# Attention on one core: loads in chunks of 4 heads over a ring of 8, value loads from ScalarE's queue, smaller and later stores

## The chip, the cores and the metric

The kernel runs on one core of a Trainium2 chip. A core has five engines with instruction streams of their own: TensorE (PE) multiplies matrices into PSUM, VectorE (DVE) and ScalarE (ACT) read PSUM and SBUF, GpSimd (POOL) works on SBUF, and SyncE (SP) here only sends DMAs. They meet through semaphores. DMAs are sent by an engine's queue and carried out by 16 DMA engines that all queues share. The metric is the device time of one execution in microseconds (us), as a median over runs.

## The reference

```python
B, H, Sq, Sk, D = 16, 32, 192, 1024, 128          # all bf16
scores = jnp.einsum("bhqd,bhkd->bhqk", q, k) * D ** -0.5
p = softmax(scores, axis=-1)
out = jnp.einsum("bhqk,bhkd->bhqd", p, v)
```

There are 512 independent heads. Each has 192 queries, 1024 keys and 1024 values of 128 elements. In bytes: a head's keys and its values are 262 KB each, its queries and its output 49 KB each; the whole problem moves 318.8 MB.

## The kernel before

**Units.** Two heads form a pair, and a pair is worked off as three units of 128 query rows: the first 128 queries of head a (k3 = 0), the first 128 of head b (k3 = 1), and the last 64 of both together (k3 = 2, two matmuls side by side in the array). That makes 256 pairs and NU = 768 units. `PPG` is the number of pairs in a group of G = 16 heads (8), `UPG` the number of units (24), and there are NGR = 32 groups.

**Stages of a unit u.** QK (`qk`, L215 to L228): two times 512 keys into a PSUM tile `s_ps`. Row maximum (`rowmax`, L300, VectorE): it writes the negated scaled scores to `ss` in SBUF and their minimum to `nb`. Then the route of the unit decides: for k3 = 0 and 1 (route W) GpSimd subtracts the minimum (`shift`, L188) into `x_sb`, and the exponential is taken later; for k3 = 2 (route EA) ScalarE takes the exponential (`exp_first`, L356) into `x_sb` and sums the row. Eight transposes on TensorE (`tr`, L244) put `x_sb` into a PSUM tile `pt_ps`. ScalarE evacuates it into `pt_sb` (`evac`, L367 with the exponential for route W, L369 as a copy for route EA). PV (`pv`, L267 to L281) multiplies by the values into `o_ps`; for route W further matmuls with a column of ones sum the rows (L270). After a pair's third unit VectorE normalises (`onorm`, L327, L330) into `ob`.

**Order.** The order on each engine is written out by hand as a loop over steps, with a lag for each stage: `LAGS=(2, 4, 5, 7)` are L_X, L_TR, L_EV, L_PV. In step s TensorE does QK of unit s + 1, the transposes of unit s - 4, and PV of unit s - 7; ScalarE evacuates unit s - 5 and then does `exp_first` of unit s - 2. Two tiles each of `s_ps`, `pt_ps` and `o_ps` fill PSUM. So the transposes of unit u wait for the evacuation of unit u - 2, and an evacuation waits for the transposes of its unit and for PV of unit u - 4 (`s_pv`, through the NPT = 4 slots of `pt_sb`).

**Loads and stores.** All DMAs are sent by SP (lines 133 to 174). `kt`, `qt` and `vs` each have NS = 2 slots of 16 heads. `loads(g)` sends three DMAs: the keys through a transposing DMA (L141), the queries through another (L144), and the values as a plain load (L149, runs of 2 KB). From the third group on, L141 waits until QK has finished with the group two before (`s_qk`), and L149 until PV has (`s_pv`). `stores(g)` waits until the 8 pairs of a group are normalised (`s_on`) and sends three stores: the first 128 rows of each head (L158), and the last 64 rows of the even and of the odd heads (L163, L164). `ob` has NSO = 2 slots of 16 heads, and `onorm` waits for the store that used the slot before. SP's order is loads of groups 0 and 1, and then for each g: loads of g + 2, stores of g. TensorE waits for the keys and the queries at the first QK of a group (L203, L204) and for the values at its first PV (L251).

Of the kernel before, what the change touches and what calls it, by code (L numbers as in the profile page):

```python
# [5 lines left out]
BF16 = mybir.dt.bfloat16  # L6
# [4 lines left out]
R_EA = 0  # L11
R_ED = 1
R_W = 2


def _attention_kernel(nc, q, k, v, out, G=16, NS=2, LAGS=(2, 4, 5, 7), ROUTES=(R_W, R_W, R_EA)):
    B, H, SQ, D = q.shape
    SK = k.shape[2]
    assert D == 128 and SK == 1024 and SQ == 192, (D, SK, SQ)
    NH = B * H  # L20
    assert NH % G == 0 and G % 2 == 0
    NGR = NH // G
    PPG = G // 2
    UPG = 3 * PPG
    NU = NGR * UPG
    KT_TILES = SK // 128
    scale = float(D) ** -0.5

# [2 lines left out]
    NSS = L_X + 2  # L31
    NX = L_TR - L_X + 2
    NPT = L_PV - L_EV + 2
    NSO = 2
    NRS = 4

    qf = q.rearrange("b h s d -> (b h) s d")
# [25 lines left out]
    with ExitStack() as es:  # L63
        def sb(name, shape, dt):
            return es.enter_context(nc.sbuf_tensor(name, shape, dt))
# [4 lines left out]
        def sem(name):  # L70
            return es.enter_context(nc.semaphore(name))

        kt = sb("kt", [128, NS, G * SK], BF16)
        qt = sb("qt", [128, NS, G * SQ], BF16)
        vs = sb("vs", [128, NS, G, KT_TILES, 128], BF16)
        ob = sb("ob", [128, NSO, PPG, 4, 128], BF16)
        ss = sb("ss", [128, NSS, SK], F32)
        nb = sb("nb", [128, NSS], F32)
        x_sb = sb("x_sb", [128, NX, SK], BF16)
# [6 lines left out]
        pt_ps = [ps("pt_ps%d" % i, [128, KT_TILES, 128], BF16) for i in range(2)]  # L86
        o_ps = [ps("o_ps%d" % i, [128, 4, 128], F32) for i in range(2)]
        s_setup = sem("s_setup")
        sxk = [sem("sxk%d" % i) for i in range(NS)]
        sxq = [sem("sxq%d" % i) for i in range(NS)]  # L90
# [15 lines left out]
        def unit_info(u):  # L106
            pr = u // 3
            k3 = u % 3
            g = pr // PPG
            pg = pr % PPG  # L110
            return pr, k3, g, pg

        O_SLOT = (0, 2, 1)

        def load_cnt(g):
            return 16 * (g // NS + 1)

        def store_cnt(g):
            return 48 * (g // NSO + 1)
# [12 lines left out]

        @block.sync
        def _(e):
            def loads(g):
                s = g % NS
                last_u = (g - NS + 1) * UPG - 1
                h0 = g * G
                if g >= NS:
                    e.wait_ge(s_qk, last_u + 1)  # L140
                e.dma_start_transpose(  # L141
                    kt[:, s], kf[h0:h0 + G].rearrange("g k d -> (g k) d")
                ).then_inc(sxk[s], 16)
                e.dma_start_transpose(  # L144
                    qt[:, s], qf[h0:h0 + G].rearrange("g k d -> (g k) d")
                ).then_inc(sxq[s], 16)
                if g >= NS:
                    e.wait_ge(s_pv, last_u + 1)
                e.dma_start(  # L149
                    vs[:, s], vf[h0:h0 + G].rearrange("g (p t) d -> p g t d", t=KT_TILES)  # L150
                ).then_inc(svl[s], 16)

            def stores(g):
                so = g % NSO
                e.wait_ge(s_on, (g + 1) * PPG)
                h0 = g * G
                og = of[h0:h0 + G]
                e.dma_start(  # L158
                    og[:, 0:128, :].rearrange("h p d -> p h d"),
                    ob[:, so].rearrange("p pg (x y) d -> p (pg x) (y d)", y=2)[:, :, 0:128],  # L160
                ).then_inc(sst[so], 16)
                oab = og[:, 128:192, :].rearrange("(pg x) p d -> x p pg d", x=2)
                e.dma_start(oab[0], ob[0:64, so, :, 1, :]).then_inc(sst[so], 16)  # L163
                e.dma_start(oab[1], ob[64:128, so, :, 1, :]).then_inc(sst[so], 16)  # L164

            for g in range(min(NS, NGR)):
                loads(g)
            for g in range(NGR):
                if g + NS < NGR:
                    loads(g + NS)  # L170
                stores(g)
            for so in range(min(NSO, NGR)):
                n_uses = len(range(so, NGR, NSO))
                e.wait_ge(sst[so], 48 * n_uses)

        @block.gpsimd
# [21 lines left out]
        def _(pe):  # L198
            def qk(u):
                pr, k3, g, pg = unit_info(u)  # L200
                s = g % NS
                if u % UPG == 0:
                    pe.wait_ge(sxk[s], load_cnt(g))  # L203
                    pe.wait_ge(sxq[s], load_cnt(g))  # L204
                if u >= 2:
                    pe.wait_ge(s_max, u - 1)
                S = s_ps[u % 2]
                a = 2 * pg
                b = 2 * pg + 1
                ins = None  # L210
                for c in range(2):
                    cs = slice(512 * c, 512 * c + 512)
                    if k3 < 2:
                        x = a if k3 == 0 else b
                        ins = pe.matmul(  # L215
                            S[:, cs],
                            qt[:, s, x * SQ: x * SQ + 128],
                            kt[:, s, x * SK + 512 * c: x * SK + 512 * c + 512],
                            start=True, stop=True,
                        )  # L220
# [13 lines left out]
                ins.then_inc(s_qk, 1)  # L234
# [12 lines left out]
            def pv(u):  # L247
                pr, k3, g, pg = unit_info(u)
                s = g % NS
                if u % UPG == 0:  # L250
# [44 lines left out]
        def _(dve):  # L295
# [15 lines left out]
            ri_total = [0]  # L311

            def onorm(pr):
                g = pr // PPG
                pg = pr % PPG
                so = g % NSO
                dve.wait_ge(s_pv, 3 * pr + 3)
                if pg == 0 and g >= NSO:
# [29 lines left out]
        def _(act):  # L348
# [13 lines left out]
            def evac(u):  # L362
                act.wait_ge(s_tr, u + 1)
                if u >= NPT:
                    act.wait_ge(s_pv, u - NPT + 1)
                if route(u) == R_W:
                    act.activation(pt_sb[:, u % NPT], pt_ps[u % 2][:], ACT_FN.Exp, scale=-1.0).then_inc(s_eva, 1)  # L367
                else:
                    act.activation(pt_sb[:, u % NPT], pt_ps[u % 2][:], ACT_FN.Copy).then_inc(s_eva, 1)  # L369

            for step in range(NU + L_EV + 1):
                u = step - L_EV
                if 0 <= u < NU and route(u) != R_ED:
                    evac(u)
                u = step - L_X
                if 0 <= u < NU and route(u) != R_W:
                    exp_first(u)
# [38 lines left out]
```

## Time and profile before

| | |
|---|---|
| median of 3 runs | 1265.64 us (1265.32 to 1267.57) |
| profiled execution, first to last instruction | 1263.1 us |
| between the two | 2.5 us |
| TensorE busy | 1234.2 us (98%) |
| VectorE busy | 1102.0 us (87%) |
| ScalarE busy | 1048.6 us (83%) |
| GpSimd busy | 960.4 us (76%) |
| granted TensorE clock, mean | 0.999 of full speed |
| DMA, mean over the span | 255 GB/s |

The page gives the span of the profiled execution, not its whole device time, so sums in this document are made against the span, and the 2.5 us between it and the median of the runs are carried over unchanged.

A row of instructions reads: line, engine, operation, output tile and input, shape and count, then busy time, mean duration, and the idle time of the engine ahead of it with what ended it. `PEld` is TensorE's loading of weights, which overlaps its matmuls. In a timeline the first column is the start and the second the duration, both in us from the start of the span; `x8` says that eight instructions are merged. Rows of `SPq` are SP's queue: the duration is how long the issue of the DMA held the queue, not the time until the data have landed. In the table of windows the columns are: window, length, busy time of PE, PEld, DVE, ACT and POOL with their instruction counts, TensorE's granted clock, DMA share (sum of packet times over 16 engines; over 1 where packets overlap), and GB/s.

### The profile page before, as it was taken

What the parts mean: (1) busy time and instruction counts of PE and PEld (TensorE: products, weight loads), DVE (VectorE), ACT (ScalarE), POOL (GpSimd) and SP (SyncE); (2) the same over time, 40 slices, a digit from 0 to 9 for tenths busy, and PEclk for the clock granted to TensorE, in tenths of its full rate; (3) what the DMA queues carried; (4) which work ended last, traced back from release to release, by engine and by line L of the source; (5) the groups of instructions that cost most, each with busy time, mean ns of one, the idle gap of its engine ahead of it and who ended that gap; (6) DMA issues with size and microseconds to landing.
All of it is one profiled execution on the core that took longest, in us unless ns stands there. A gap on an engine that the chain in (4) does not pass through costs nothing.

```text
span 1263.1 us, 48658 instructions
## 1 busy us (share of the span) xinstructions
PE 1234.2 (98%) x20480; PEld 1009.4 (80%) x20480; DVE 1102.0 (87%) x2304; ACT 1048.6 (83%) x1281; POOL 960.4 (76%) x518
## 2 busy tenths in 40 slices
PE   3999999999999999999999999999999999999997
PEld 1888888888888888888888888888888888888886
DVE  2889888898988989898898988889898898989885
ACT  1888888888888888888888888888888888888886
POOL 2778777777877778787777877777787777878774
PEclk9999999999999999999999999999999999999999
DMA  9999999999999999999999999999999999999941
GB/s 288 268 261 240 278 280 266 288 270 245 254 269 261 279 233 255 281 275 262 261 230 272 271 276 268 252 251 272 272 267 281 253 263 252 271 261 281 244 118 27
DMA packets 790743, 321.89 MB, mean 255 GB/s; under 512 B 724992, under 2 KB 724992, under 8 KB 790528
## 3 DMA queue, kind: packets, MB, share of 16 engines
q1 hardware_dynamic: 790528, 318.78, 108.8%
q8 instruction: 164, 2.69, 0.8%
q14 instruction: 51, 0.42, 0.1%
HBM read 134.22 MB, written 25.17 MB: 126 GB/s over the span
## 4 chain that ended last, share of the span: by engine, by line
PE 97%; SPq 1%; DMA 1%; ACT 0%; issue 0%; DVE 0%; ACTq 0%
PE pt_ps L244 33%; PE o_ps L267 24%; PE s_ps L215 18%; PE o_ps L273 11%; PE s_ps L222 9%; SPq L141 1%; DMA vs<-in_v_dram 1%; PE o_ps L270 1%; PE o_ps L275 1%; SPq L144 0%; PE s_ps L228 0%; ACT x_sb L356 0%; ACT pt_sb L367 0%; DVE ob L330 0%; DVE rinv L327 0%
## 5 line engine op out<-in xcount | busy, mean ns | idle before, releaser
L188 POOL TENSOR_TENSOR x_sb<-ss,nb 128x1024 bf16<-128x1024 f32 x512 | 959.7, 1895 | 288.9 <-PE pt_ps L244 266.8
L300 DVE TENSOR_SCALAR_CACHE_REDUCE ss<-s_ps 128x1024 f32<-128x1024 f32 x768 | 938.5, 1222 | 140.5 <-PE s_ps L215 110.8
L244 PEld LDWEIGHTS pt_ps<-ident,x_sb 128*128 128x128 bf16 x6144 | 487.1, 148 | 203.3 <-issue 105.4
L367 ACT ACTIVATE pt_sb<-pt_ps 128x1024 bf16<-128x1024 bf16 x512 | 521.0, 1018 | 41.9 <-PE pt_ps L244 41.8
L244 PE MATMUL pt_ps<-ident,x_sb 128*128 128x128 bf16 x6144 | 520.7, 228 | 0.2 <-ACT pt_sb L367 0.2
L267 PE MATMUL o_ps<-vs,pt_sb 128*128 128x128 bf16 x4096 | 403.0, 217 | 0.3 <-DMA vs<-in_v_dram 0.3
L369 ACT ACTIVATE pt_sb<-pt_ps 128x1024 bf16<-128x1024 bf16 x256 | 262.1, 1024 | 140.1 <-PE pt_ps L244 140.0
L270 PE MATMUL o_ps<-ones,pt_sb 128*128 128x1 bf16 x4096 | 376.0, 165 | 0.0
L267 PEld LDWEIGHTS o_ps<-vs,pt_sb 128*128 128x128 bf16 x4096 | 352.3, 97 | 0.5 <-DMA vs<-in_v_dram 0.4
L270 PEld LDWEIGHTS o_ps<-ones,pt_sb 128*128 128x128 bf16 x4096 | 340.7, 96 | 0.0
L215 PE MATMUL s_ps<-kt,qt 128*128 128x512 bf16 x1024 | 305.3, 379 | 21.3 <-DMA qt<-in_q_dram 21.0
L356 ACT ACTIVATE x_sb<-ss,nb 128x1024 bf16<-128x1024 f32 x256 | 292.3, 1142 | 23.6 <-DVE ss L300 23.6
L273 PE MATMUL o_ps<-vs,pt_sb 128*64 128x128 bf16 x2048 | 162.3, 222 | 0.0
L275 PE MATMUL o_ps<-vs,pt_sb 128*64 128x128 bf16 x2048 | 162.3, 222 | 0.0
L222 PE MATMUL s_ps<-kt,qt 128*64 128x512 bf16 x512 | 153.2, 381 | 0.6 <-DVE ss L300 0.5
L228 PE MATMUL s_ps<-kt,qt 128*64 128x512 bf16 x512 | 153.2, 381 | 0.0
L330 DVE TENSOR_TENSOR ob<-o_ps,rinv 128x384 bf16<-128x384 f32 x256 | 142.7, 557 | 8.7
L273 PEld LDWEIGHTS o_ps<-vs,pt_sb 128*64 128x64 bf16 x2048 | 121.0, 109 | 17.1
L275 PEld LDWEIGHTS o_ps<-vs,pt_sb 128*64 128x64 bf16 x2048 | 121.0, 109 | 0.0
L215 PEld LDWEIGHTS s_ps<-kt,qt 128*128 128x128 bf16 x1024 | 63.3, 96 | 23.6 <-issue 21.5
L300 DVE DVE_READ_ACCUMULATOR ss<-s_ps 128x1 f32 x768 | 64.0, 83 | 0.0
L356 ACT ACTIVATION_READ_ACCUMULATOR x_sb<-ss,nb 128x1 f32 x256 | 48.9, 191 | 0.0
(11 smaller groups left out, 165.7 us busy)
## 6 DMA issues: line engine op xcount, KB each, us to landing
vs<-in_v_dram SPq DMA_DIRECT2D x32, 4096.0 KB, 15.2
out_dram<-ob SPq DMA_DIRECT2D x32, 512.0 KB, 15.9
out_dram<-ob SPq DMA_DIRECT2D x64, 128.0 KB, 4.9
kt<-in_k_dram SPq DMA_TRANSPOSE x32, 21.4
qt<-in_q_dram SPq DMA_TRANSPOSE x32, 6.6
```

The lines of the kernel that those rows point to most:

```text
L188: gp.tensor_tensor(x_sb[:, u % NX, :], ss[:, u % NSS, :], nb[:, u % NSS: u % NSS + 1].to_broadcast([128, SK]), ALU.subtract,).then_inc(s_x ...
L215: ins = pe.matmul(S[:, cs], qt[:, s, x * SQ: x * SQ + 128], kt[:, s, x * SK + 512 * c: x * SK + 512 * c + 512], start=True, stop=True,)
L222: pe.matmul(S[0:64, cs], qt[:, s, a * SQ + 128: a * SQ + 192], kt[:, s, a * SK + 512 * c: a * SK + 512 * c + 512], start=True, stop=True, ...
L244: ins = pe.transpose(PT[:, t, :], X[:, t: SK: KT_TILES], ident[:])
L267: ins = pe.matmul(O[:, sl, :], PTS[:, t, :], vs[:, s, x, t, :], start=first, stop=last, skip_group_check=True)
L270: ins = pe.matmul(O[:, 3, sl: sl + 1], PTS[:, t, :], ones[:, 0:1], start=False, stop=last, skip_group_check=True)
L273: pe.matmul(O[0:64, sl, :], PTS[:, t, 0:64], vs[:, s, a, t, :], start=first, stop=last, skip_group_check=True, tile_position=(0, 0))
L275: ins = pe.matmul(O[64:128, sl, :], PTS[:, t, 64:128], vs[:, s, b, t, :], start=first, stop=last, skip_group_check=True, tile_position=(0, ...
L300: dve.tensor_scalar(ss[:, u % NSS, :], s_ps[u % 2][:], -scale, None, ALU.mult, ALU.min, accum_out=nb[:, u % NSS: u % NSS + 1],).then_inc(s ...
L356: act.activation(x_sb[:, u % NX, :], ss[:, u % NSS, :], ACT_FN.Exp, bias=nb[:, u % NSS: u % NSS + 1], scale=-1.0, accum_out=rs[:, pr % NRS ...
L367: act.activation(pt_sb[:, u % NPT], pt_ps[u % 2][:], ACT_FN.Exp, scale=-1.0).then_inc(s_eva, 1)
L369: act.activation(pt_sb[:, u % NPT], pt_ps[u % 2][:], ACT_FN.Copy).then_inc(s_eva, 1)
```

## The change

The slots become smaller and more: chunks of CH = 4 heads (PPC = 2 pairs, UPC = 6 units) in a ring of NS = 8 slots, so the buffers are as large as before (32 heads), and there are NCH = 128 chunks. Keys and queries of a chunk are still sent by SP, now counted on one semaphore per slot; from chunk 8 on, SP waits until QK has finished with chunk c - 8. Values are sent by ScalarE, between its evacuation and its `exp_first` in a step: chunk c < 8 at step 3(c - 1), at least 0, without a wait; a later chunk at step 6(c - 7) + 8, directly behind the evacuation that waited for the same count of `s_pv`. Stores are for SG = 8 heads (PPS = 4 pairs) with a ring of NSO = 3; SP sends a store group after the load of a chunk once the chunk it waited for lies far enough behind the pairs of the group, and the remaining groups after the last load. TensorE's wait for keys and queries is one wait every 6 units, that for values likewise.

```diff
-def _attention_kernel(nc, q, k, v, out, G=16, NS=2, LAGS=(2, 4, 5, 7), ROUTES=(R_W, R_W, R_EA)):
+def _attention_kernel(nc, q, k, v, out, CH=4, NS=8, SG=8, NSO=3, LAGS=(2, 4, 5, 7), ROUTES=(R_W, R_W, R_EA)):
...
-        kt = sb("kt", [128, NS, G * SK], BF16)
-        qt = sb("qt", [128, NS, G * SQ], BF16)
-        vs = sb("vs", [128, NS, G, KT_TILES, 128], BF16)
-        ob = sb("ob", [128, NSO, PPG, 4, 128], BF16)
+        kt = sb("kt", [128, NS, CH * SK], BF16)
+        qt = sb("qt", [128, NS, CH * SQ], BF16)
+        vs = sb("vs", [128, NS, CH, KT_TILES, 128], BF16)
+        ob = sb("ob", [128, NSO, PPS, 4, 128], BF16)
...
         @block.sync
         def _(e):
-            def loads(g):
-                s = g % NS
-                last_u = (g - NS + 1) * UPG - 1
-                h0 = g * G
-                if g >= NS:
-                    e.wait_ge(s_qk, last_u + 1)
+            def load_kq(c):
+                s = c % NS
+                h0 = c * CH
+                if c >= NS:
+                    e.wait_ge(s_qk, (c - NS + 1) * UPC)
                 e.dma_start_transpose(
-                    kt[:, s], kf[h0:h0 + G].rearrange("g k d -> (g k) d")
-                ).then_inc(sxk[s], 16)
+                    kt[:, s], kf[h0:h0 + CH].rearrange("g k d -> (g k) d")
+                ).then_inc(sx[s], 16)
                 e.dma_start_transpose(
-                    qt[:, s], qf[h0:h0 + G].rearrange("g k d -> (g k) d")
-                ).then_inc(sxq[s], 16)
-                if g >= NS:
-                    e.wait_ge(s_pv, last_u + 1)
-                e.dma_start(
-                    vs[:, s], vf[h0:h0 + G].rearrange("g (p t) d -> p g t d", t=KT_TILES)
-                ).then_inc(svl[s], 16)
+                    qt[:, s], qf[h0:h0 + CH].rearrange("g k d -> (g k) d")
+                ).then_inc(sx[s], 16)
...
-            for g in range(min(NS, NGR)):
-                loads(g)
-            for g in range(NGR):
-                if g + NS < NGR:
-                    loads(g + NS)
-                stores(g)
+            done = 0
+            for c in range(NCH):
+                load_kq(c)
+                while done < NSG and UPC * (c - NS + 1) >= 3 * PPS * (done + 1) + L_PV + 2:
+                    stores(done)
+                    done += 1
+            while done < NSG:
+                stores(done)
+                done += 1
...
-                if u % UPG == 0:
-                    pe.wait_ge(sxk[s], load_cnt(g))
-                    pe.wait_ge(sxq[s], load_cnt(g))
+                if u % UPC == 0:
+                    pe.wait_ge(sx[s], 2 * load_cnt(g))
...
+            def load_v(c):
+                s = c % NS
+                if c >= NS:
+                    act.wait_ge(s_pv, (c - NS + 1) * UPC)
+                act.dma_start(
+                    vs[:, s],
+                    vf[c * CH:(c + 1) * CH].rearrange("g (p t) d -> p g t d", t=KT_TILES),
+                ).then_inc(svl[s], 16)
+
+            v_at = {}
+            for c in range(NCH):
+                at = 3 * (c - 1) if c < NS else (c - NS + 1) * UPC - 1 + NPT + L_EV
+                v_at.setdefault(max(at, 0), []).append(c)
+
             for step in range(NU + L_EV + 1):
                 u = step - L_EV
                 if 0 <= u < NU and route(u) != R_ED:
                     evac(u)
+                for c in v_at.get(step, ()):
+                    load_v(c)
                 u = step - L_X
                 if 0 <= u < NU and route(u) != R_W:
                     exp_first(u)
```

More of the change, by code (lines that the diff above doesn't have):

```diff
@@ L20, in _attention_kernel @@
     NH = B * H
[L21 to L25, printed above, removed]
+    assert NH % CH == 0 and CH % 2 == 0 and SG % CH == 0 and NH % SG == 0
+    NCH = NH // CH
+    PPC = CH // 2
+    UPC = 3 * PPC
+    NU = NCH * UPC
+    NSG = NH // SG
+    PPS = SG // 2
+    CPS = SG // CH
     KT_TILES = SK // 128
@@ L33, in _attention_kernel @@
     NPT = L_PV - L_EV + 2
-    NSO = 2
     NRS = 4
@@ L88, in _attention_kernel @@
         s_setup = sem("s_setup")
-        sxk = [sem("sxk%d" % i) for i in range(NS)]
-        sxq = [sem("sxq%d" % i) for i in range(NS)]
+        sx = [sem("sx%d" % i) for i in range(NS)]
         svl = [sem("svl%d" % i) for i in range(NS)]
@@ L108, in unit_info, with load_cnt @@
             k3 = u % 3
-            g = pr // PPG
-            pg = pr % PPG
-            return pr, k3, g, pg
+            return pr, k3, pr // PPC, pr % PPC
         O_SLOT = (0, 2, 1)
-        def load_cnt(g):
-            return 16 * (g // NS + 1)
+        def load_cnt(c):
+            return 16 * (c // NS + 1)
         def store_cnt(g):
@@ L134, in _ @@
         def _(e):
-            def loads(g):
-                s = g % NS
-                last_u = (g - NS + 1) * UPG - 1
-                h0 = g * G
-                if g >= NS:
-                    e.wait_ge(s_qk, last_u + 1)
+            def load_kq(c):
[3 more added lines that the diff above has]
+                    e.wait_ge(s_qk, (c - NS + 1) * UPC)
                 e.dma_start_transpose(
-                    kt[:, s], kf[h0:h0 + G].rearrange("g k d -> (g k) d")
-                ).then_inc(sxk[s], 16)
+                    kt[:, s], kf[h0:h0 + CH].rearrange("g k d -> (g k) d")
+                ).then_inc(sx[s], 16)
                 e.dma_start_transpose(
-                    qt[:, s], qf[h0:h0 + G].rearrange("g k d -> (g k) d")
-                ).then_inc(sxq[s], 16)
-                if g >= NS:
-                    e.wait_ge(s_pv, last_u + 1)
-                e.dma_start(
-                    vs[:, s], vf[h0:h0 + G].rearrange("g (p t) d -> p g t d", t=KT_TILES)
-                ).then_inc(svl[s], 16)
+                    qt[:, s], qf[h0:h0 + CH].rearrange("g k d -> (g k) d")
+                ).then_inc(sx[s], 16)
             def stores(g):
                 so = g % NSO
-                e.wait_ge(s_on, (g + 1) * PPG)
-                h0 = g * G
-                og = of[h0:h0 + G]
+                e.wait_ge(s_on, (g + 1) * PPS)
+                h0 = g * SG
+                og = of[h0:h0 + SG]
                 e.dma_start(
@@ L164, in stores @@
                 e.dma_start(oab[1], ob[64:128, so, :, 1, :]).then_inc(sst[so], 16)
-            for g in range(min(NS, NGR)):
-                loads(g)
-            for g in range(NGR):
-                if g + NS < NGR:
-                    loads(g + NS)
-                stores(g)
-            for so in range(min(NSO, NGR)):
-                n_uses = len(range(so, NGR, NSO))
+            done = 0
[7 more added lines that the diff above has]
+                done += 1
+            for so in range(min(NSO, NSG)):
+                n_uses = len(range(so, NSG, NSO))
                 e.wait_ge(sst[so], 48 * n_uses)
@@ L249, in pv @@
                 s = g % NS
-                if u % UPG == 0:
+                if u % UPC == 0:
                     pe.wait_ge(svl[s], load_cnt(g))
@@ L313, in onorm @@
             def onorm(pr):
-                g = pr // PPG
-                pg = pr % PPG
+                g = pr // PPS
+                pg = pr % PPS
                 so = g % NSO
```

## The prediction

> **What bounds the kernel now.** I read the page's busy shares and chain first, then the waits, the chain in order of time, the timeline of SP's queue, the throughput by windows, and last ScalarE's timeline in the steady state.
>
> ```profile
> span 1263.1 us, 48658 instructions
> PE 1234.2 (98%) x20480; PEld 1009.4 (80%) x20480; DVE 1102.0 (87%) x2304; ACT 1048.6 (83%) x1281; POOL 960.4 (76%) x518
> PE 97%; SPq 1%; DMA 1%; ACT 0%; issue 0%; DVE 0%; ACTq 0%
> ```
>
> TensorE is the chain. Is any of its time spent waiting for loads? The chain in order of time answers:
>
> ```profile
> 56.70 0.65 PE pt_ps L244 x8
> ...
> 1160.70 0.65 PE pt_ps L244 x8
> ```
>
> The two transposes stand 1104.00 us apart, which is 230 x 4.80: a pair of heads (three units) takes 4.80 us, also across every group boundary. TensorE never stops for a load in there; 256 pairs are 1228.8 us. So only the two ends of the span can get shorter: 1263.1 - 1228.8 = 34.3 us.
>
> The start, in the view of waits and in SP's timeline:
>
> ```profile
> PE s_ps L215 <- DMA qt<-in_q_dram: 21.0, 1, 21.0
> ```
>
> ```profile
> 0.80 14.90 SPq L141 DMA_TRANSPOSE kt<-in_k_dram  x1
> 15.76 3.07 SPq L144 DMA_TRANSPOSE qt<-in_q_dram  x1
> 18.87 0.59 SPq L149 DMA_DIRECT2D vs<-in_v_dram  x1
> 19.52 28.54 SPq L141 DMA_TRANSPOSE kt<-in_k_dram  x1
> ...
> 125.50 0.59 SPq L149 DMA_DIRECT2D vs<-in_v_dram  x1
> 126.14 4.29 SPq L158 DMA_DIRECT2D out_dram<-ob  x1
> 130.47 9.78 SPq L163 DMA_DIRECT2D out_dram<-ob  x1
> ```
>
> TensorE sits 21.0 us until the queries of 16 heads have landed. The issue of a transposing load lasts as long as its data needs: 14.90 us for the keys of 16 heads. Row 19.52 lasts 28.54, which is 14.90 plus the 13.6 us until 33.1 in which the values ahead of it in the queue were still moving; the stores behind values (4.29 and 9.78 us) are held up the same way. The value load itself always takes 0.59 us, though it follows transposes. The end:
>
> ```profile
> 1257.46 0.38 SPq L158 DMA_DIRECT2D out_dram<-ob  x1
> 1257.88 1.13 SPq L163 DMA_DIRECT2D out_dram<-ob  x1
> 1259.06 1.29 SPq L164 DMA_DIRECT2D out_dram<-ob  x1
> ```
>
> VectorE's last result ends at 1257.43; the stores of the last 16 heads take the remaining 5.7 us. Rates, by windows (last column GB/s; keys alone, then values at full rate):
>
> ```profile
> 5.00:8.00 3.00, 0.00 (x0) 0.00 (x0) 0.00 (x0) 0.00 (x0) 0.00 (x0) 1.00 1.28 290
> 24.00:28.00 4.00, 3.59 (x11) 0.57 (x10) 3.98 (x9) 1.24 (x2) 4.00 (x3) 1.00 1.04 397
> ```
>
> **The change, part by part.**
>
> *First chunk on the path.* Keys of 4 heads instead of 16. Two rows give a line: 16384 rows in 14.90 us and 3072 rows in 3.07 make 0.34 us fixed and 0.89 us per 1000 rows. Keys of a chunk (4096 rows): 3.98 us; queries (768): 1.02 us. From the end of the query issue to the first matmul took 21.01 - 18.83 = 2.18 us. The first matmul would start at 0.80 + 3.98 + 0.05 + 1.02 + 2.18 = 8.0 us if nothing else moved.
>
> But ScalarE now sends value chunks 0, 1 and 2 at once: their steps (0, 0 and 3) come before its first activation that waits. That is 3.15 MB beside the 1.25 MB of chunk 0's keys and queries; before, values came after them. If the values were all served first, at 395 GB/s, they would add 8.0 us: first matmul at 16.0. If both queues move equal bytes, 2.49 MB at about 340 GB/s (between the two windows) are 7.3 us instead of 1.25 MB at 290 = 4.3: add 3.0. I take 11.0, the even share, as no row shows two queues side by side. Gain 21.0 - 11.0 = **10.0 us**, ends 5.0 and 13.0. The filling of the pipeline behind it stays: before, the first PV matmul (12.2 us after the first QK) waited at most 0.4 us for values, and they now come earlier.
>
> *Next chunks.* From then on a chunk needs 1.25 MB (keys, queries) and 1.05 MB (values) per two pairs, 9.6 us: 239 GB/s, and a store share of 0.2 MB makes it 260. One queue in series made 290 to 397. SP sends chunks 1 to 7 without a wait, so the keys run ahead. Cost 0 as long as the values, sent every three units (4.8 us), don't starve the keys; with the cover gone, each late chunk costs what it is late.
>
> *Steady state, SP's queue.* Before, 6 DMAs per 16 heads; now 8 key and query loads and 6 stores on SP, 4 value loads on ScalarE's queue: 192 DMAs become 448 + 128. Per chunk SP issues 3.98 + 1.02 = 5.0 us, and in every second one a store group. The last stores above, with nothing ahead, are 2.8 us for 16 heads; 8 heads take 1.4 to 2.8. So SP uses 5.0 to 7.8 of 9.6 us. A load is sent seven chunks, 67 us, before use, so a late issue is hidden. Stores two chunks late: the ring of three store buffers asks for the first result of group g about 23 units (37 us) after the load that precedes the store of g - 3; SP needs under 10 us for both. Cost 0; gone if SP runs over 30 us late.
>
> *Steady state, ScalarE's queue.* This is the added wait. Its wait on s_pv is already met: the evacuation just ahead of it waits for the same count. What the issue holds up is the next evacuation (k3 = 1), for which TensorE's transpose two units on waits. ScalarE's timeline, then TensorE's transposes, in one pair:
>
> ```profile
> 600.19 1.01 ACT L367 ACTIVATE pt_sb<-pt_ps 128x1024 bf16<-128x1024 bf16 x1
> 601.36 1.02 ACT L367 ACTIVATE pt_sb<-pt_ps 128x1024 bf16<-128x1024 bf16 x1 [0.15 <-PE pt_ps L244]
> 602.94 1.02 ACT L369 ACTIVATE pt_sb<-pt_ps 128x1024 bf16<-128x1024 bf16 x1 [0.55 <-PE pt_ps L244]
> ```
>
> ```profile
> 599.03 0.71 PE L244 MATMUL pt_ps<-ident,x_sb 128*128 128x128 bf16 x8
> 600.67 0.66 PE L244 MATMUL pt_ps<-ident,x_sb 128*128 128x128 bf16 x8
> ```
>
> The issue stands behind the evacuation that ends at 601.20. The next would end at 602.38, and the transpose that needs it comes at 599.03 + 4.80 = 603.83: 1.45 us of slack, and 0.15 us idle before, so an issue of up to 1.6 us costs TensorE nothing. ScalarE is idle 0.70 us per pair, 1.40 per chunk, so it also catches up. Bounds for one issue: 0 (beside the evacuation) and 9.8 us (L163, the longest row of an issue that is held). I take 0.59, the value load's own row. Cost **0**; 128 issues at 9.8 us would be 128 x 8.2 = 1050 us.
>
> On that price a rule speaks against the change. The rows that bear on it: every issue behind moving values was held (4.29, 9.78, 28.54), all on one queue. The Trainium skill, "Perfetto Trace Analysis", section "DMA Instruction — HWDGE (DVE, Sync)", says the descriptor generator is shared and locked by one instruction at a time, so that a value load from ScalarE could wait for the whole of a transposing load on SP, though the queues differ. By it the five value loads (chunks 3 to 7) that fall in SP's opening burst would each wait up to a key issue, 3.98 us, and cost, as an estimate, at most 5 x (3.98 + 0.59 - 1.6) = 15 us, more than the gain; by the row 0.59 nothing. No run here shows two queues.
>
> In the steady state the phase helps: SP starts a chunk at about 599.2 in such a cycle (QK of k3 = 2), and the value load follows the evacuation that ends at 606.00, 6.8 us later; SP's loads take 5.0.
>
> *Tail.* The last store group has 8 heads: 2.8 us of issues become 1.4. I take **1.5 us**; ends 0 (issues not shorter) and 2.4 (half of the 786 KB at 160 GB/s, as the end of the span moved them).
>
> **Sum.** 10.0 + 1.5 = 11.5 us: span 1263.1 - 11.5 = 1251.6. The median of the runs, 1265.64, stands 2.5 us over the span, so 1254.1. Ends: 13.0 + 2.4 gives 1250.2, 5.0 + 0 gives 1260.6.
>
> **Rivals.**
> 1. *The start gives its gain back*: values crowd out keys of chunks 0 to 3, or ScalarE's issues are held during SP's burst. For: 3 MB of values at once, and SP's issues lasting as long as the data. Against: 290 to 397 GB/s against 260 needed. A start of 16.0 and 5 us more of late keys or held issues: nothing is left of 10.0, 1.5 at the tail: 1264; range 1259 to 1267.
> 2. *ScalarE is held in the steady state* (slower). In every second chunk SP's stores follow its loads; if ScalarE's issue can't pass them, it goes only when SP is done. It decides from 607.6 on: SP at work for over 7.8 us after 599.2, plus 0.59. With steady rows, keys 17.94/4 = 4.5, queries 4.0/4 = 1.0 and stores 2.8, SP frees at 607.5, the issue ends at 608.1, 0.5 late; about 60 such chunks make 30 us: 1284. A hold over 0.2 us late already eats the 11.5. For: the held rows. Against: the 0.59 right after transposes.
> 3. *Transfers become the bound* (slower): the queue's cycle for 16 heads was 36.8 us (140.96 to 177.74) against TensorE's 38.4. If values still moved in series with transposes and each of 12 more DMAs added 0.38 us (the shortest row), it would be 41.4: 3.0 x 32 = 96 us, 1350. Against: values leave the queue that they blocked for 14 us a group.
>
> **How the numbers follow.** Forecast 0.72 (own range 1250 to 1261); rival 1 0.10; rival 2 0.14; rival 3 0.04. The range takes in the forecast and rival 1, 1249 to 1266, and leaves out rivals 2 and 3, 0.18. Within 0.2% (2.5 us, about what a measurement of this kernel can tell) lies a third of rival 1: faster 0.78, same 0.04, slower 0.18.
>
> **What would show it.** Right: the wait of L215 for qt falls from 21.0 to 8 to 16 us; transposes keep 4.80 us per pair; value issues on ScalarE's queue near 0.6 us; the last store ends about 4 us after the last VectorE result. Wrong: transposes waiting for pt_sb, a wait of QK for qt or kt after the first, value issues over 1.6 us, pairs longer than 4.80.

## The result, and the profile after

The changed kernel takes 1394.39 us (median of 4 runs, 1390.45 to 1397.96) where the kernel before takes 1265.48 on the same chip: a ratio of 1.101, with an interval of 1.099 to 1.103. It is 10% slower; the forecast was 1254.0 with a range to 1266. The profiled execution spans 1392.2 us, against 1263.1.

The page of the kernel after (span and busy shares, two of the rows in 40 slices, the shares of the chain):

```profile
span 1392.2 us, 49169 instructions
PE 1268.5 (91%) x20480; PEld 1029.1 (74%) x20480; DVE 1104.2 (79%) x2304; ACT 1048.9 (75%) x1281; POOL 960.6 (69%) x518
...
PE   4557889899899999979998999998999899989898
...
PEclk9778899999999999989999999999999999999999
...
PE 79%; SPq 11%; DMA 7%; DVE 2%; issue 1%; ACT 0%; DVEq 0%; ACTq 0%
```

SP's queue and DMAs, 2% of the chain before, are 18% of it now. In slices of 34.8 us TensorE is no longer full: the first four are four to seven tenths busy (the first holds the start itself), and later ones dip. Its granted clock fell from 0.999 to 0.956. The chain in order of time shows a pair at 4.80 us as before (312.68 to 317.48), and then one of the dips:

```profile
312.68 0.65 PE pt_ps L239 x8
317.48 0.65 PE pt_ps L239 x8
...
341.73 0.65 PE pt_ps L239 x8
346.65 0.92 SPq L139
347.62 1.28 SPq L142
348.94 1.48 SPq L151
351.15 6.14 DMA out_dram<-ob
358.11 1.24 DVE ss L295 x2
359.39 1.04 PE s_ps L210 x2
```

SP sends the keys (L139) and queries (L142) of a chunk, and only then the first store (L151) of its group. The store lands at 357.3; `onorm` (L322) needed the slot that it empties at 351.2. VectorE stands, the row maxima behind `onorm` stand, and so TensorE's next scores do. The waits say how often (us in total, times, longest):

```profile
DVE rinv L322 <- DMA out_dram<-ob: 76.1, 13, 16.0
...
PE s_ps L210 <- DVE ss L295: 62.3, 14, 14.9
PE s_ps L210 <- DMA qt<-in_q_dram: 41.9, 3, 16.9
```

So there are two faults: late stores all through, and three waits for keys and queries (16.9 before the first matmul, the others in the opening). Why, shows in SP's queue over the opening:

```profile
0.80 12.39 SPq L139 DMA_TRANSPOSE kt<-in_k_dram  x1
13.24 1.26 SPq L142 DMA_TRANSPOSE qt<-in_q_dram  x1
14.55 4.24 SPq L139 DMA_TRANSPOSE kt<-in_k_dram  x1
...
20.16 4.12 SPq L139 DMA_TRANSPOSE kt<-in_k_dram  x1
...
25.64 13.77 SPq L139 DMA_TRANSPOSE kt<-in_k_dram  x1
39.46 5.76 SPq L142 DMA_TRANSPOSE qt<-in_q_dram  x1
45.25 18.22 SPq L139 DMA_TRANSPOSE kt<-in_k_dram  x1
...
64.84 17.87 SPq L139 DMA_TRANSPOSE kt<-in_k_dram  x1
```

The issue of the keys of 4 heads takes 4.1 to 4.2 us while no values move, and 12 to 18 us while they do: value chunks 0 to 2 move until 13.1, chunks 3 to 7 (sent at 26.5 to 41.0) until 62.7. The DMA packets from 2 to 6 us, by queue (packets, MB, share of the engines), say how they share:

```profile
q10 hardware_dynamic: 546, 1.09, 77.7%
q1 hardware_dynamic: 504, 0.13, 14.4%
```

q10 carries the values in packets of 2 KB, q1 the keys in packets of 256 B. The two queues move nearly the same number of packets, so the values go at 272 GB/s and the keys at 32. The Trainium skill, "DMA: Bandwidth & Descriptors", section "Queues, rings and completion order", says that a DMA engine goes round between the queues it has work for, a packet at a time; equal counts agree with it. A packet on that page holds several descriptors, and these counts do not show whether a turn is one of the profile's packets.

In the steady state SP's queue is full and late, and the rows look like this:

```profile
397.04 7.09 SPq L139 DMA_TRANSPOSE kt<-in_k_dram  x1
404.18 1.28 SPq L142 DMA_TRANSPOSE qt<-in_q_dram  x1
405.50 0.58 SPq L151 DMA_DIRECT2D out_dram<-ob  x1
406.14 0.63 SPq L156 DMA_DIRECT2D out_dram<-ob  x1
406.81 3.52 SPq L157 DMA_DIRECT2D out_dram<-ob  x1
410.37 4.84 SPq L139 DMA_TRANSPOSE kt<-in_k_dram  x1
```

Here the two queues mostly move one after the other. The value load sent at 402.62 moves nothing until SP has issued the queries at 405.46: from 402.7 to 405.4 us only the keys' queue has packets, from 405.7 to 407 only the values' queue.

```profile
402.62 0.37 ACTq L370 DMA_DIRECT2D vs<-in_v_dram  x1
```

```profile
q1 hardware_dynamic: 3060, 0.78, 127.5%
...
q10 hardware_dynamic: 256, 0.52, 103.4%
```

From 200 us on, 72 of 109 value loads begin to move within 0.35 us of the end of SP's query issue, a median of 3.3 us after they were sent. The issue of a chunk's keys takes a median of 4.98 us when almost no values move meanwhile (50 issues), and 7.43 us when most of a value load does (56 issues).

A load of keys goes out a median of 21.6 us after QK has freed its slot (2.4 before; between 300 and 1100 us, taking QK's end as the start of the last row maximum). It still lands 36 us ahead of its use; the stores queued behind it have no such lead.

The other queue and the end answer to the last parts of the prediction. Value loads on ScalarE (size, median us to landing), and the last store group:

```profile
vs<-in_v_dram ACTq DMA_DIRECT2D x128, 1024.0 KB, 7.9
```

```profile
1388.48 0.38 SPq L151 DMA_DIRECT2D out_dram<-ob  x1
1388.91 0.60 SPq L156 DMA_DIRECT2D out_dram<-ob  x1
1389.55 0.62 SPq L157 DMA_DIRECT2D out_dram<-ob  x1
```

**Where the time went.** The starts of the 768 row maxima split the span; TensorE alone needs 1.6 us per unit, 38.40 us per 16 heads. The same four parts serve for every run below.

| us | before | after | difference |
|---|---|---|---|
| first row maximum | 22.1 | 17.9 | -4.2 |
| lost up to unit 78, against 1.6 us per unit | -2.0 | 57.7 | +59.7 |
| lost from unit 78 to 762 | 0.0 | 75.5 | +75.5 |
| after VectorE's last result | 5.7 | 3.8 | -1.9 |
| span | 1263.1 | 1392.2 | +129.1 |

In the opening, by chunk: 16.6, 1.7 and 16.8 us are lost before chunks 3, 4 and 5 for keys, and 15.9 and 6.3 at chunks 7 to 8 and 11 to 12 for stores (the first store group, its results ready at 65.5, is sent at 138.67 behind the loads of chunk 11, which QK's free slot would have allowed at 70.3).

### The profile page after: what moved, and what is told of

The parts are those of the page before. It is cut to its first block, busy times and chain, and to the rows that moved or that the text cites. A ratio compares the mean times of both kernels' runs of the same rounds, so it can differ in the third digit from the quotient of the medians.

```text
span 1392.2 us, 49169 instructions
## 1 busy us (share of the span) xinstructions
PE 1268.5 (91%) x20480; PEld 1029.1 (74%) x20480; DVE 1104.2 (79%) x2304; ACT 1048.9 (75%) x1281; POOL 960.6 (69%) x518
## 4 chain that ended last, share of the span: by engine, by line
PE 79%; SPq 11%; DMA 7%; DVE 2%; issue 1%; ACT 0%; DVEq 0%; ACTq 0%
PE pt_ps L239 27%; PE o_ps L262 19%; PE s_ps L210 15%; PE o_ps L268 9%; PE s_ps L217 7%; SPq L139 6%; DMA out_dram<-ob 6%; SPq L142 2%; SPq L156 2%; DVE ss L295 1%; DMA qt<-in_q_dram 1%; PE o_ps L265 1%; SPq L151 1%; PE o_ps L270 0%; DVE rinv L322 0%
## 5 line engine op out<-in xcount | busy, mean ns | idle before, releaser
L239 PEld LDWEIGHTS pt_ps<-ident,x_sb 128*128 128x128 bf16 x6144 | 494.7, 149 | 216.4 <-issue 122.4
L239 PE MATMUL pt_ps<-ident,x_sb 128*128 128x128 bf16 x6144 | 531.1, 231 | 2.7 <-issue 2.4
L262 PE MATMUL o_ps<-vs,pt_sb 128*128 128x128 bf16 x4096 | 407.8, 218 | 4.9 <-issue 4.8
L210 PE MATMUL s_ps<-kt,qt 128*128 128x512 bf16 x1024 | 313.3, 388 | 104.4 <-DVE ss L295 62.3
L265 PE MATMUL o_ps<-ones,pt_sb 128*128 128x1 bf16 x4096 | 380.4, 166 | 2.1 <-issue 2.1
L262 PEld LDWEIGHTS o_ps<-vs,pt_sb 128*128 128x128 bf16 x4096 | 356.1, 98 | 0.4 <-issue 0.2
L351 ACT ACTIVATE x_sb<-ss,nb 128x1024 bf16<-128x1024 f32 x256 | 292.0, 1141 | 17.9 <-DVE ss L295 17.9
L270 PE MATMUL o_ps<-vs,pt_sb 128*64 128x128 bf16 x2048 | 168.4, 227 | 4.2 <-issue 4.2
L268 PE MATMUL o_ps<-vs,pt_sb 128*64 128x128 bf16 x2048 | 168.2, 227 | 0.3 <-issue 0.3
L217 PE MATMUL s_ps<-kt,qt 128*64 128x512 bf16 x512 | 158.5, 392 | 0.6 <-DVE ss L295 0.5
L223 PE MATMUL s_ps<-kt,qt 128*64 128x512 bf16 x512 | 158.5, 393 | 0.0
L268 PEld LDWEIGHTS o_ps<-vs,pt_sb 128*64 128x64 bf16 x2048 | 125.5, 112 | 18.5 <-issue 2.2
L270 PEld LDWEIGHTS o_ps<-vs,pt_sb 128*64 128x64 bf16 x2048 | 125.6, 112 | 4.7 <-issue 4.7
L322 DVE RECIPROCAL rinv<-o_ps 128x2 f32<-128x2 f32 x256 | 42.7, 167 | 96.9 <-DMA out_dram<-ob 76.1
```

The source lines that it names most:

```text
L210: ins = pe.matmul(S[:, cs], qt[:, s, x * SQ: x * SQ + 128], kt[:, s, x * SK + 512 * c: x * SK + 512 * c + 512], start=True, stop=True,)
L217: pe.matmul(S[0:64, cs], qt[:, s, a * SQ + 128: a * SQ + 192], kt[:, s, a * SK + 512 * c: a * SK + 512 * c + 512], start=True, stop=True, ...
L239: ins = pe.transpose(PT[:, t, :], X[:, t: SK: KT_TILES], ident[:])
L262: ins = pe.matmul(O[:, sl, :], PTS[:, t, :], vs[:, s, x, t, :], start=first, stop=last, skip_group_check=True)
L265: ins = pe.matmul(O[:, 3, sl: sl + 1], PTS[:, t, :], ones[:, 0:1], start=False, stop=last, skip_group_check=True)
L268: pe.matmul(O[0:64, sl, :], PTS[:, t, 0:64], vs[:, s, a, t, :], start=first, stop=last, skip_group_check=True, tile_position=(0, 0))
```

## The experiments

Four theories were on record at first. A: two queues at once hurt (values crowd out the keys). B: small pieces make the transfers slower, whatever the queue. C: the ring of three small store groups is too short. D: only the opening makes a backlog that is then carried along. Two more came after the first results. S: each change between transposing and plain transfers in a queue costs time. P: each transposing DMA has a fixed price. A time with no interval is that of a single execution; the losses are worked out from the profiled one.

**The two parts alone.** e1 takes the value loads out of ScalarE's block and puts them back on SP, behind the keys and queries of their chunk:

```diff
+            def load_v(c):                       # in the block of SP
+                if c >= NS:
+                    e.wait_ge(s_pv, (c - NS + 1) * UPC)
+                e.dma_start(vs[:, c % NS], ...)
...
                 load_kq(c)
+                load_v(c)
```

> The changed kernel with one thing undone: the value load of each chunk is sent by SP again, right behind the chunk's keys and queries; chunks of 4, ring of 8 and the store ring stay. Theory A (two queues: the 256-byte packets of the transposing loads take turns with the 2 KB packets of the values, and the sum moves less than one queue in series): first matmul at 8 to 9 us, transposing key loads back to about 4.2 us each, no waits for stores, 1252 to 1258 us. Theory B (granularity: more and smaller DMAs cost the time): stays above 1350. Theory C (three store slots of 8 heads, sent late, are too few): the start gains, the 76 us of waits for stores stay, about 1310. Theory D (the values sent in the opening put SP 75 us behind, and it never recovers): 1252 to 1258 as by A, since values follow their keys.

Measured: 1481.36 us, a ratio of 1.168 (1.164 to 1.172). The start is good (first row maximum 9.4), the opening loses 49.3, the steady state 181.5: 44.77 us per 16 heads. All in one queue, the keys behind the values of the chunk before take 7.1 to 8.3 us to issue (395 to 448 us), and the stores come late 53 times:

```profile
DVE rinv L332 <- DMA out_dram<-ob: 216.4, 53, 37.9
```

So the small pieces are the larger fault, and ScalarE's queue softens it. e2 is the kernel before with only the value loads sent from ScalarE, the first two not before the queries of their group have landed:

```diff
-                if g >= NS:                      # in the block of SP
-                    e.wait_ge(s_pv, last_u + 1)
-                e.dma_start(vs[:, s], ...)
+            def load_v(g):                       # in the block of ScalarE, behind the evacuation
+                if g < NS:                       # that waits for the same count
+                    act.wait_ge(sxq[g], 16)
+                else:
+                    act.wait_ge(s_pv, (g - NS + 1) * UPG)
+                act.dma_start(vs[:, g % NS], ...)
```

> The kernel before with one thing done: halves of 16 heads as before, but values sent by ScalarE, the first two only when the queries of their half have landed (so no opening burst). A: key loads beside values need well over the 18 us of before, the group's cycle goes over 38.4 us, total above 1300. B, C and D: within 1% of 1265, as neither chunks, nor stores, nor the opening have changed.

Measured: 1291.59 us, 26 more than before; opening +14.7, steady state +11.0. From 88 to 91 us the two queues again move equal numbers of packets (512 and 511):

```profile
q10 hardware_dynamic: 511, 1.05, 89.4%
q1 hardware_dynamic: 512, 0.13, 19.2%
```

Keys and queries land only a median of 3.9 us ahead of their use, against 12.5 before. Theory A has a price of its own, 26 us with large pieces; B carries more. The two do not add up: small pieces alone (e1) cost 216 us, both together 129.

**The stores.** e3 gives `ob` a fourth slot, e8 makes the store groups as large as before:

```diff
-CH=4, NS=8, SG=8, NSO=3
+CH=4, NS=8, SG=8, NSO=4        # e3
+CH=4, NS=8, SG=16, NSO=2       # e8
```

> The changed kernel with NSO = 4 store slots instead of 3 (32 heads, as many as before). C: the 76 us of waits for stores go, 1392 becomes 1316 or less. A and B: transfers stay too slow, the waits shrink by less than half and partly move to keys and queries: 1345 to 1390. D: the opening stays, 1320 to 1390.

> The changed kernel with store groups of 16 heads in two slots (before's size) instead of 8 in three; chunks and ScalarE's value queue stay. S: one change from stores to transposing loads fewer per 16 heads, about 2 us of 40.6: 38.5 us, so TensorE nearly keeps pace after the opening, 1310 to 1340. If stores are not part of it: 1380 to 1395.

Measured: 1389.99 and 1398.02 us. e3 loses 33.0 in the opening in place of 57.7, but 95.3 in the steady state in place of 75.5. The lag of the loads behind their free slot grows from 21.6 to 43.8 us and their lead shrinks from 36 to 16: the longer ring gives a queue that is too slow more room to fall behind. e8 loses 48.0 in the opening and 87.1 in the steady state. C is not the cause; late stores are where the lateness shows. e8 also speaks against S where stores are concerned: it leaves out a change from stores to transposing loads per 16 heads, for which S gave 38.5 us, and it takes 41.45.

**The opening.** e4 asks for values only as they are needed, and for the first only when the first keys have landed:

```diff
-                if c >= NS:
+                if c == 0:
+                    act.wait_ge(sx[0], 32)
+                elif c >= NS:
                     act.wait_ge(s_pv, (c - NS + 1) * UPC)
...
-                at = 3 * (c - 1) if c < NS else (c - NS + 1) * UPC - 1 + NPT + L_EV
-                v_at.setdefault(max(at, 0), []).append(c)
+                v_at.setdefault(UPC * c, []).append(c)
```

> The changed kernel with the value loads still on ScalarE's queue, but each sent just in time, one per six steps (chunk c at step 6c, the first after its keys and queries have landed): no burst in the opening. First matmul at about 8 us by all. D: nothing else is wrong, 1252 to 1260. A: SP's cycle for two chunks stays over 19.2 us in the steady state, waits for stores come later but come: above 1290. B: above 1300.

Measured: 1337.65 us. The first row maximum comes at 10.1, no later chunk waits over 0.3 us for keys and queries, and the 22.7 us lost in the opening are one wait of `onorm` for the first store (22.6). Yet the steady state still loses 61.7 (40.56 us per 16 heads), so D explains the opening and not the rest. The packets show a part of it: the DMA engines stand still between transfers, here between the packets of stores and those of a transposing load whose issue began at 204.97. The windows of e4 (last column GB/s):

```profile
207.50:208.00 0.50, 0.50 (x7) 0.43 (x7) 0.35 (x3) 0.50 (x1) 0.50 (x1) 1.00 7.11 175
208.00:210.00 2.00, 1.29 (x23) 1.06 (x22) 2.00 (x4) 1.21 (x2) 0.97 (x1) 1.00 0.09 1
210.00:210.50 0.50, 0.50 (x9) 0.43 (x8) 0.50 (x1) 0.00 (x0) 0.00 (x0) 1.00 0.13 22
```

Two us pass with 1 GB/s while work is queued (ScalarE sends a value load at 208.34, too). The kernel after has such holes too (8 GB/s from 409 to 410). e14 adds the fourth store slot to e4:

```diff
-SG=8, NSO=3
+SG=8, NSO=4        # and the change of e4
```

> The chunked kernel with values just in time on ScalarE's queue and, in addition, four store slots of 8 heads instead of three. With three slots it lost 23 us in chunk 7 to 8, waiting for the first store, which SP sends only behind the load of chunk 11. If the late first store is a loss of its own: these 23 us go and the steady 40.56 us per 16 heads stay, 1312 to 1316. If the loads behind it are late anyway: the wait moves to keys and queries, 1325 to 1336.

Measured: 1328.78 us. The 23 us at chunk 7 went, 13.4 came back at chunk 9, and the steady state is as slow (65.5 lost).

**Size and order of the pieces.** e6 is e1 with chunks of 8 heads, e12 is e4 with chunks of 8 (`CH=8, NS=4` in both). e5 sends the pieces of e1, from chunk 4 on, grouped by kind: keys and queries of four chunks, then values of four chunks, then two store groups, with four store slots. In its list, K, V and S are a load of keys and queries, a load of values, and a store group.

```diff
-CH=4, NS=8
+CH=8, NS=4         # e6: values on SP as in e1; e12: values as in e4
```

```diff
+            if b + 2 < NCH // 4:                 # e5, all on SP
+                ops += [("K", c0 + i, 1) for i in range(4)]
+                ops += [("V", c0 + i, 1) for i in range(4)]
+            ops += [("S", g, 0) for g in (2 * b, 2 * b + 1)]
```

> All on SP's queue, chunks of 8 heads in a ring of 4, keys and queries, values, stores of 8 heads in turn: 4 changes of kind per 16 heads instead of 8 (2 before), 12 DMAs instead of 18 (6 before). S: 36.8 + 8.6 x 2/6 = 39.7 us per 16 heads, 1300. P: halfway, 41.1 us, 1345.

> Values just in time on ScalarE's queue, as in the run of that kind, but chunks of 8 heads in a ring of 4. With chunks of 4 the steady state took 40.56 us per 16 heads. If small transposing DMAs and changes of kind are the cost, half the excess over 38.4 goes: 39 to 39.5 us, 1290 to 1310. If two queues are the cost by themselves: still 40.5 us, 1335.

> All on SP's queue, the same small DMAs as in the run with the values on SP (chunks of 4, ring of 8), but from chunk 4 on in the order four times keys and queries, four value loads, two store groups of 8 heads (four store slots so that both fit). So the number and size of loads is that of the chunked kernel (45.4 us for 16 heads when kinds alternate) and the number of changes between transposing and plain DMAs that of the kernel before (36.8 us). Theory S (every change of kind costs dead time on the DMA engines): 37 to 38.4 us per 16 heads, TensorE bound again, 1255 to 1270. Theory P (every DMA has a fixed cost, whatever stands beside it): still about 44 us, 1435. Both by the gaps seen in the packets (0.6 us for each of six more transposing DMAs, no more changes): 40.4 us, 1325.

| | us | us per 16 heads in the steady state |
|---|---|---|
| before: 16 heads, one queue | 1265.5 | 38.40 (bound by TensorE; its queue needs 38.06, see below) |
| e6: 8 heads, one queue | 1317.64 | 39.66 |
| e1: 4 heads, one queue | 1481.36 | 44.77 |
| e5: 4 heads, one queue, by kind | 1336.75 | 40.86 |
| e12: 8 heads, two queues, just in time | 1291.36 | 39.01 |
| e4: 4 heads, two queues, just in time | 1337.65 | 40.56 |

The dose is clear on one queue and on two. e5 moves the same pieces as e1 and is 145 us faster. Of its cycle:

```profile
399.82 4.22 SPq L154 DMA_TRANSPOSE kt<-in_k_dram  x1
...
405.41 5.41 SPq L154 DMA_TRANSPOSE kt<-in_k_dram  x1
...
425.99 3.21 SPq L165 DMA_DIRECT2D vs<-in_v_dram  x4
...
441.61 4.47 SPq L154 DMA_TRANSPOSE kt<-in_k_dram  x1
```

Its queue takes 41.8 us for these 16 heads. Per 16 heads e1 goes from transposing to plain and back four times, e5 once: (44.77 - 40.86) / 6 is 0.65 us for each of the six changes left out, an inferred price, since e5 has a store slot more as well (which alone, in e3, did not help). So S holds between loads of the two kinds, and what remains of e5 over the kernel before speaks for P. Two runs part P from the number of DMAs as such: the kernel before with only its keys and queries in pieces of 4 heads (e9), or with only its values in pieces (e10), in the order and with the stores of before.

```diff
+                ops += [("K", c0 + i, kn) for i in range(0, 4, kn)]
+                ops += [("V", c0 + i, vn) for i in range(0, 4, vn)]
+            # e9: kn = 1, vn = 4; e10: kn = 4, vn = 1; one store group of 16 heads behind
```

> The kernel before (SP alone, groups and stores of 16 heads, the same opening), with one edit from the third group on: a group's keys and queries are sent as four pairs of transposing DMAs of 4 heads instead of one pair of 16; the value load and the stores stay whole, and no change of kind is added. If a transposing DMA has a fixed cost of about 0.6 us: 6 more per group, 36.8 + 3.6 = 40.4 us, over TensorE's 38.4, 1325 to 1330. If only changes of kind cost: 1263 to 1268.

> The counterpart: the kernel before with, from the third group on, a group's values sent as four plain loads of 4 heads behind one another; keys, queries and stores whole. If plain loads behind one another add next to nothing: 1263 to 1268. If any small DMA costs: 3 more at 0.6 us, 38.6 us per group, about 1270.

Measured: e9 1363.22 us, e10 1267.59. In e9 the opening is that of before (22.1, -1.7), and the whole loss is a steady cycle of 41.83 us in which TensorE now waits for values:

```profile
PEld o_ps L284 <- DMA vs<-in_v_dram: 76.4, 29, 6.9
```

What the queue of the kernel before needs is read where it runs behind. From 140.96 to 978.34 SP issues with no gap over 0.44 us, while its lag behind the freed slot shrinks from 7.0 us to nothing:

```profile
140.96 17.55 SPq L141 DMA_TRANSPOSE kt<-in_k_dram  x1
...
978.34 19.67 SPq L141 DMA_TRANSPOSE kt<-in_k_dram  x1
```

These are 22 cycles of 38.06 us on average (36.2 to 41.2), only 0.34 under TensorE's 38.40. Six more transposing DMAs per 16 heads raise this to 41.83: 0.63 us each (0.57 if 38.40 is taken as the start). Three more plain DMAs make 38.50, or 0.15 us each; they do eat slack (the keys' lag grows from 2.4 to 12.1 us). So P holds for transposing DMAs, but no single price fits: e5 sends as many of them as e9, and three value loads and three stores more, in 40.86 us.

**Keeping the early start alone.** The first row maximum can come 8 to 13 us earlier (14.0 to 8.8 in these runs, 22.1 before). e7, e11 and e13 are the kernel before with pieces of 8 heads in the opening only, all on SP:

A triple is the kind, the first chunk of 4 heads, and how many chunks go in one load.

```diff
-            for g in range(min(NS, NGR)):
-                loads(g)
+        ops = [('K', 0, 2), ('V', 0, 2), ('K', 2, 2), ('V', 2, 2), ('K', 4, 2), ('K', 6, 2), ('V', 4, 4)]   # e7, e11
+        ops = [('K', 0, 2), ('V', 0, 2), ('K', 2, 2), ('V', 2, 2), ('K', 4, 2), ('V', 4, 4), ('K', 6, 2)]   # e13
...
+                kn = 2 if b + 2 <= 5 else 4                    # e11: keys of groups 2 to 5 in halves, too
```

> The kernel before (SP alone, groups of 16 heads, stores of 16) with only the opening in smaller pieces: group 0 as two halves of 8 heads, each keys, queries, values; group 1 as keys and queries of 8 heads twice, then its values. First matmul at 12 to 13 us instead of 21.0 by all. S and P: the opening's later pieces land just in time, 1256 to 1262 in all. If the gain is given back by group 1 or 2 landing late: 1263 to 1267.

> The run with the opening in halves gained 8.5 us at the first matmul and lost 7.7 again by group 2, whose keys landed late. Here the keys and queries of groups 2 to 5 are sent as halves too, so that the first half lands earlier; the rest as before. If the late group was the only loss: 1255 to 1258. If the added DMAs eat what they bring (1.2 us per group): 1262 to 1268.

> The kernel before with the opening in pieces on SP's one queue, reordered: halves of 8 heads for group 0 (keys and queries, values, keys and queries, values); for group 1 keys and queries of 8 heads, then all its values, then keys and queries of the other 8 heads, which meet those of group 2 without a change of kind. In the run in halves TensorE lost 9.7 us in chunk 5 because group 1's values landed at 71.4 us, behind both halves of its keys; here they should land at about 58. If that was the only loss: first matmul at 12.6 us and kept, 1256 to 1259. If the added transposing DMAs and changes make group 2 late instead: 1262 to 1268.

Measured against before in the same sessions: e7 1267.83 us, ratio 1.0022 (1.0012 to 1.0031); e11 1271.47, 1.0049 (1.0032 to 1.0066); e13 1265.34, 1.0003 (0.9992 to 1.0015). In all three the first row maximum comes at 13.6 to 14.0 in place of 22.1, and from chunk 5 on that is lost again. In e7 one wait does it, for the values of the second group, which land at 71.4:

```profile
PEld o_ps L284 <- DMA vs<-in_v_dram: 8.3, 1, 8.3
```

In e13 those values land at 62.0, and the second half of the group's keys and queries, now behind them, lands at 72.3; TensorE loses 4.1, 0.9 and 1.2 us at chunks 5, 6 and 11, and no longer for values. A stream that needs 38.06 us of TensorE's 38.40 gains 0.34 us per group, and the opening asks for more DMAs and an earlier finish at once. No version was found that beats the kernel before.

## Why the prediction was wrong

**First chunk** (first matmul at 11.0, ends 8 to 16): the first matmul came at 16.9, past the end "values all served first". The even share of bytes was the wrong choice; an even share of packets, 2 KB against 256 B, is nearly the values-first case. Gain 4.2 us by the first row maximum, not 10.0.

**Next chunks: cost 0.** This step failed, and cost 35 of the 59.7 us that the opening lost. It compared 260 GB/s needed with the 290 to 397 of one queue, as if the mean said who is served. The cover it named, that the values don't starve the keys, was gone: keys of chunks 3 to 5 were issued in 13.8 to 18.2 us for 3.98, and the three chunks came 35 us late in sum (16.6, 1.7 and 16.8). In e4, with the values asked for later, that loss is gone. The other 22 us of the opening are the first stores behind late loads, the failure of the next step.

**Steady state, SP's queue: cost 0.** This step failed and cost 75.5 us. Three terms were too small.
- "5.0 to 7.8 of 9.6 us" took 3.98 us for keys with nothing beside them. In the steady state their issue has a median of 6.84 (4.98 almost without values, 7.43 beside a value load), since the values of ScalarE's queue use the same DMA engines. The step priced the queue and left out the engines behind it. The Trainium skill has the rule, in "DMA: Bandwidth & Descriptors", section "Issuing engines are not separate DMA queues": transfers sent by different engines end on the same 16 and interleave.
- The line for a transposing DMA, 0.34 us fixed, was drawn through two rows alone in the queue. Behind one another and with no values moving, keys and queries of 4 heads take 5.61 us (14.55 to 20.16), where a quarter of 16 heads' 17.97 is 4.5. That is 1.1 us for one and a half DMAs more per chunk, or 0.75 us each by these rows; 0.63 by e9.
- The changes of kind, 0.65 us each as inferred from e1 and e5, had no term.

By the packet records (quarters of a us under 100 GB/s count as dead), the DMA engines stood 5.6 us per 16 heads before and 7.9 after, and moved 302 and 294 GB/s else: with 9.96 MB per 16 heads this makes 38.6 and 41.8 us, against 38.40 and 41.05 by TensorE's units. It splits the same time and is not a second measurement; most of the difference is time in which the DMA engines stand. In e9 they stand 7.5 us, though no change of kind was added there.

The cover named, "gone if SP runs over 30 us late", was too long as well. The ring asks for its slot some 38 us after the freed slot, about as worked out (37). But from the start of the load to the landing of the store behind it 16 to 28 us passed ahead of the late stores, where the prediction had under 10 for the issues and nothing for the landing. So stores were late at load lags of 20 to 27 us. And the queue had little room to begin with: 0.34 us per 16 heads, as its back-to-back rows in the kernel before show.

**ScalarE's queue: cost 0.** Right for TensorE. The issues took 0.37 to 0.53 us, none over 1.6, and TensorE's transposes wait for `pt_sb` once, 0.2 us, as before. The rule weighed against it, from the Trainium skill's "Perfetto Trace Analysis", section "DMA Instruction — HWDGE (DVE, Sync)", has a descriptor generator held by one instruction at a time. The issue rows do not show it: value issues stayed at 0.37 to 0.44 us in the steady state beside key issues of 4 to 14. The packets agree with it: 72 of 109 value loads moved only when SP's pair of transposing loads had been issued. In e12, with larger key loads, 6 of 55 did so, so whether the generator or the DMA engines held them is open. TensorE did not wait for it; SP's queue paid. (The 0.59 us that the value load "always" takes in the kernel before has two exceptions in 32, 1.29 and 1.67.)

**Tail: 1.5 us.** Right: 5.7 became 3.8, a gain of 1.9.

**The rivals.** What happened is rival 3, transfers become the bound, with a chance of 0.04 and a price of 41.4 us per 16 heads; measured were 41.05. Its condition, values still in series with transposes, holds in effect at the DMA engines, and the argument against it, that values leave the queue that they blocked, was the error: they left the queue and not the engines. That the figures lie so close is luck: its sum starts from a queue cycle of 36.8 us, one of the short ones, where the mean is 38.06, and adds 0.38 us for each of 12 DMAs, where six transposing ones alone cost 0.63 each in e9. It still gave 1350 and not 1394, since the opening of rival 1 comes on top, with 59.7 us in place of "nothing is left of 10.0". Rival 2 did not occur. Of the signs named, a wait of QK for queries after the first came true (two of the three waits), and so did pairs longer than 4.80; the first wait fell to 16.9 us and not to 8 to 16.

## What to carry to other kernels

A load stream that uses 38.06 of 38.40 us has no room for more DMAs: before cutting loads into pieces, find the mean cycle of the queue over a stretch in which it runs behind, and add a price per transposing DMA (here 0.6 to 0.75 us) and per change between transposing and plain loads (here about 0.65). A second queue ends on the same DMA engines: with groups of 16 heads it cost 26 us (e2), with chunks of 4 it saved 4.2 of 44.8 us per 16 heads (e4 against e1). Where both queues move at once, as in the opening, 256-byte packets beside 2 KB packets get about a tenth of the bytes. Stores queued behind prefetches inherit the queue's whole lateness, though the prefetches themselves hide it.

## What the hardware showed that was not expected

- **A stop costs more than its length.** After the stop at 351 the granted clock (third column from the end) stays at half for some 7 us:

```profile
357.00:359.00 2.00, 0.00 (x0) 0.00 (x0) 1.59 (x4) 0.00 (x0) 0.00 (x0) 0.58 1.27 288
359.00:361.00 2.00, 1.61 (x10) 1.08 (x10) 2.00 (x5) 0.00 (x0) 0.00 (x0) 0.50 1.21 233
361.00:363.00 2.00, 2.00 (x23) 1.07 (x21) 1.34 (x5) 1.68 (x2) 1.57 (x1) 0.50 0.95 155
363.00:365.00 2.00, 2.00 (x28) 1.82 (x27) 1.38 (x3) 1.29 (x3) 1.04 (x2) 0.72 1.24 234
365.00:367.00 2.00, 2.00 (x34) 1.74 (x32) 1.35 (x3) 1.22 (x2) 1.18 (x1) 1.00 1.19 306
```

  By the starts of the transposes, VectorE's wait of 6.17 us loses 5.6 us at once and 1.7 in the two steps behind it, 7.3 in all. Over the steady state, eleven such waits for stores are 54 us, and the stops they make 67 of the 75.5 lost; that the clock makes up the difference was not tested by a run of its own. Another 6.6 us go at 591, where TensorE stands 4.8 us for nothing that the profile shows. The Trainium skill, "TensorE: Matmul & The Clock Gate", section "Part 1: The HAM clock gate (the "warmup" mystery)", states half clock after an idle window of about 3.4 us; the 0.50 in these rows agrees.
- **Holes between transfers** of up to 2 us (208 to 210 us in e4, at 1 GB/s), with work in both queues. Splitting the keys and queries alone (e9) raised the time in which the DMA engines stand from 5.6 to 7.5 us per 16 heads. What holds the DMA engines in them is open.
- **Even plain splitting is not free**: in e10, three more plain loads per 16 heads took 10 us of the loads' lead (12.5 to 2.4), though the span grew by only 2.8 us, little more than the runs of the kernel before spread.
